# Which of two products of the last feed-forward group is split once more, on one Trainium2 core

## The chip, the cores and the metric

The kernel runs on one core of one Trainium2 chip. The core has a matrix engine (TensorE, "PE" in the profile), a vector engine (VectorE, DVE), a scalar engine (ScalarE, ACT), GpSimd (POOL) and SyncE (SP); each runs its own instructions in order, and the engines wait for each other by semaphores. SP, POOL and ACT also issue DMA transfers (rows SPq, POOLq, ACTq). Matrix products land in PSUM, eight banks of 128 x 512 fp32 numbers; everything else lies in SBUF. The metric is the device time of one execution in microseconds.

## The reference

A block with modulated layer norms, linear attention and a gated feed-forward part, for 2048 tokens of width 1024 and a hidden width of 3584:

```python
mod = (_silu(c) @ w_mod).reshape(c.shape[0], 6, 1, -1)   # sa, ca, ga, sb, cb, gb
h = _layernorm(x, axis=-1) * (1 + ca) + sa
x = x + ga * _A_ref(h, A_wqkv, A_wo)                     # linear attention
h = _layernorm(x, axis=-1) * (1 + cb) + sb
x = x + gb * _B_ref(h, B_w_gate, B_w_up, B_w_down)       # gelu(h @ w_gate) * (h @ w_up) @ w_down
```

The change lies in the last product, with w_down (3584 x 1024), and the outputs made from it.

## The kernel before, in words

**Stages.** `kvq_phase`, `merge_phase` and `wo_phase` make the attention part. Then the feed-forward part works on two groups of 1024 tokens: `gate_up(0)`, `down_out(0)`, `gate_up(1)`, `down_out(1)`. Each product of that part is a 2 x 2 block product made from seven products of half-size blocks (the Winograd form of Strassen's scheme), so sums of blocks take the place of an eighth product.

**The seven down products.** `down_out(g)` multiplies blocks of the hidden layer (A11, A12, A21, A22 and sums of them, 14 tiles of 128 x 512 each) with blocks of w_down or sums of them, named b11, b21, b22, t0, t1, t2, t3. The sums t0 to t3 lie in DRAM (`t_scr`). A *plain* product (`plain`) has four row tiles q of 128 tokens; each takes 14 matmuls of 512 columns into bank q (0 to 3), and is followed by its output step. b11, t1, t2, t3 are accumulated in these banks one onto the other, so that bank q holds the running sum. A *nested* product (`nested`) is itself made from seven smaller ones, steps g1 to g7, each of 2 x 7 matmuls of 256 columns into one of the banks 4 to 7; ACT copies the bank to SBUF after g1, g3 and g5 (`fcopy`), since the next step accumulates onto the bank, and DVE combines the copies with other banks. The outputs come in four quadrants (row pair r, column half c) after g2 (0,0), g5 (1,1), g6 (1,0) and g7 (0,1). Nested are b21, b22, t0 in both groups, and in group 1 also t2.

**The end of group 1 before.** t2 is nested. Its outputs P7 are kept in SBUF (`p7v`, helper `c22_last`) and subtracted from `p5v` to give the output block C22. Then t3 is plain, accumulated onto the running sum in the banks 0 to 3, and `c21_out` adds `p7v` to give C21. The steps of n7 (nested t2), n3 (nested b22) and m4 (plain t3) are interleaved by hand:

```python
run(n7[0], n3[5], n7[1], n3[6], *n7[2:5])
run(m4[6], n7[5], m4[7], m4[8], n7[6], *m4[9:], *m4[:6])
```

(even entries of m4 are matmuls of a row tile, odd ones its output.) Row tile 1 is the last, in two halves of 256 columns, each with its output and its store.

**An output** (`finish`, and the `out` helpers) is three DVE operations on a 128 x 512 tile: add or subtract with the PSUM bank, multiply by the gate row, add to the residual x, which was loaded into one of two buffers (`rest`, `xio_ring`; the load waits for the stores of the buffer's previous contents). A store to DRAM follows (`store`), issued by ACT in group 1 and by POOL in group 0.

**Sums on DVE.** `sub_sums` makes the four sums of a nested product's left side. The right sides' sums are made in `gate_up`: `wd_sums` in group 0 (t1, t3 and the second-level sums of b21, b22, t0, kept in `u_scr`) and `wd_late_sums` in group 1, for the fourth nested product. They are put between the DVE work of the 14 units of `gate_up` and *paced* to it.

**What sets the order.** The code records all operations; `Plan.order` then orders each engine's instructions. TensorE keeps the recorded order. For DVE, ACT, POOL and SP a list scheduler with fixed costs sweeps forward and back 16 times and keeps the best order it finds, for the whole program at once. So an edit at the end can move instructions anywhere on these four engines. In `down_out(0)` the second of two DMA transposes that load the next group's tokens (`h2_load`) is held back until the matmuls of nested t0 are done (`plan.hold`). ScalarE scales these tokens afterwards (`h2_mod`).

Of the kernel before, what the change touches and what calls it, by code (L numbers as in the profile page):

```python
# [266 lines left out]
def kernel(  # L267
# [97 lines left out]
    def at(off, shape, dt):  # L365
        return Ring(off, shape, dt, 1)()
# [95 lines left out]
    p7v = at(88, [TT, NW], FP32)  # L462
    c0_ring = Ring(174, [TG], F16, 3)
    gl_ring = Ring(177, [TG], F16, 3)
    c1_ring = Ring(180, [TG], F16, 3)
# [52 lines left out]
    def tt_op(out, a, b, op):  # L518
        ve.tensor_tensor(out=out, in0=a, in1=b, op=op)  # L519
# [250 lines left out]
    def fcopy(ring, ps):  # L770
        t = ring()
        ac.activation(out=t, in_=ps, func=AF.Copy)  # L772
        return t
# [209 lines left out]
    def move(dst, src, add):  # L983
# [5 lines left out]
    NESTED = ("b21", "b22", "t0", "t2")  # L989
# [43 lines left out]
    def wd_late_sums(c):  # L1033

        t, u = wdt_ring(), wdu_ring()[:, 0]
        sy.dma_start(out=t, in_=wd_full["t2"][:, 2 * c:2 * c + 2, :])
# [225 lines left out]
    def gate_up(g):  # L1262
# [33 lines left out]
        for i in range(NPR):  # L1296
# [54 lines left out]
            if i + 2 < NPR:  # L1351
# [2 lines left out]
    W_AT = [{"b11": 0, "b21": (4, 5, 6, 7, 8, 9, 10), "t0": (11, 12, 13, 0, 1, 2, 3), "t1": 4,  # L1354
# [3 lines left out]

    def down_out(g):
        NC = 2  # L1360
# [19 lines left out]
        def plain(name, A, out, start):  # L1380

            wt = quarters(W_AT[g][name], [NPR, NW], F16 if name[0] == "t" else BF16)
            sy.dma_start(out=wt, in_=wd_full[name])

            def mm(q, c):
                for i in range(NPR):
                    te.matmul(psm[:, q, c], lhsT=A[:, i, q * P:(q + 1) * P], rhs=wt[:, i, c],  # L1387
                              start=(start and i == 0), stop=(i == NPR - 1), skip_group_check=True)

            steps = []  # L1390
            for q in range(TT):
                parts = 2 if last and name == "t3" and q == 1 else 1
                for n in range(parts):
                    c = slice(n * NW // parts, (n + 1) * NW // parts)
                    steps += [lambda q=q, c=c: mm(q, c), lambda q=q, c=c: out(q, psm[:, q, c], c)]
            return steps

        def sub_sums(A, S, keep, cuts):
# [8 lines left out]
                tt_op(s4, x12, s2, ALU.add)  # L1407
                tt_op(s3, x11, x21, ALU.subtract)

        def nested(name, A, S, keep, out):  # L1410


            j, x = NESTED.index(name), A.rearrange("p (k e) t -> p e k t", e=2)
            at_w = W_AT[g][name]
            dt = F16 if name[0] == "t" else BF16
            y11, y21, y22 = (quarters(at_w[n], [NPR // 2, HB], dt) for n in (0, 1, 6))
            t1, t0, t2, t3 = (quarters(at_w[n], [NPR // 2, HB], F16) for n in (2, 3, 4, 5))
            for t, src in ((y11, wd_quarter(name, 0, 0)), (y21, wd_quarter(name, 1, 0)), (t1, u_scr[:, :, j, 1, :]),
                           (t0, u_scr[:, :, j, 0, :]), (t2, u_scr[:, :, j, 2, :]), (t3, u_scr[:, :, j, 3, :]),
                           (y22, wd_quarter(name, 1, 1))):  # L1420
                sy.dma_start(out=t, in_=src)
            x11, x12, x21, x22 = (x[:, e, :, h * HB:(h + 1) * HB] for h in range(2) for e in range(2))
            s1, s2, s4 = S
            s3 = x21 if keep is None else keep
            st = {}

            def mm(b, a, y, start):
                ps = psm[:, b, :].rearrange("p (q n) -> p q n", q=2)
                for q in range(2):
                    for k in range(NPR // 2):  # L1430
                        te.matmul(ps[:, q, :], lhsT=a[:, k, q * P:(q + 1) * P], rhs=y[:, k, :],  # L1431
                                  start=(start and q == 0 and k == 0), stop=(k == NPR // 2 - 1), skip_group_check=True)
                return ps

            def g1():
                st["a"] = free.pop(0)
                st["p1"] = fcopy(sub_ring, mm(st["a"], x11, y11, True))

            def g2():
                b = free.pop(0)  # L1440
                out(0, 0, mm(b, x12, y21, True), st["p1"], ALU.add)
                free.append(b)

            def g3():
# [64 lines left out]
        def u2_out(xt):  # L1509
            def out(q, ps, c):  # L1510
                t = w12[:, q, :]
                v = p5v[:, q, :] if last else t
                tt_op(v, p5v[:, q, :], ps, ALU.subtract)
                tt_op(t, v, gbrow[:, NW:D], ALU.mult)
                tt_op(t, t, xt[:, q, :], ALU.add)
            return out

# [20 lines left out]
        def c22_last(xt):  # L1538
            def out(r, c, ps, sb, op):
                t, p7 = f16_pair(), quad(p7v, r, c)  # L1540
                if sb is None:
                    ac.activation(out=p7, in_=ps, func=AF.Copy)
                else:
                    tt_op(p7, ps, sb, op)
                tt_op(t, quad(p5v, r, c), p7, ALU.subtract)
                tt_op(t, t, gate2(1, c), ALU.mult)
                tt_op(quad(xt, r, c), t, quad(xt, r, c), ALU.add)
                if (r, c) in ((1, 0), (0, 1)):
                    store(xt, 1, 1, 2 * r, 2 * r + 2)
            return out  # L1550

        def c21_out(xt):
            def out(q, ps, c):
                finish(xt, 1, 0, q, ps, p7v[:, q, c] if last else None, ALU.add, c)
                if last:
                    store(xt, 1, 0, q, q + 1, c)
                elif q % 2:
                    store(xt, 1, 0, q - 1, q + 1)
            return out

        def run(*steps):
# [42 lines left out]
        m7 = plain("t2", A21, c22_out(xo), False)  # L1604
        t2_load = plan.ops[-1]
        plan.hold(n5_done)
        plan.ahead = 36000
        h2_load(g + 1, 1)
        plan.ahead = 14000
        plan.hold()  # L1610
        plan.pairs.append((t2_load, plan.ops[-1]))
        for f in h2_mods[g + 1][1] + h2_steps:
            f()
# [37 lines left out]
```

## Time and profile before

| | |
|---|---|
| median of 7 runs | 760.17 us (759.39 to 761.46) |
| the profiled execution | 759.93 us, of which the span of instructions is 758.1 us |
| PE busy | 742.1 us (98%), 3955 matmuls |
| DVE busy | 607.8 us (80%) |
| ACT busy | 381.2 us (50%) |
| POOL busy | 103.7 us (14%) |
| TensorE clock granted | 1.000 |
| DMA | 149.81 MB, 197 GB/s over the span |
| matmul groups at stake | L1387 (plain) x402, 86.9 us; L1431 (nested) x686, 76.8 us |

The page gives busy times, a view of the span in 40 slices, DMA queues, the chain of work that ended last, and groups of instructions. A line number such as L1431 is that of the code, L519 is the helper `tt_op` (nearly all of DVE's work), L772 the helper `fcopy`. In a row of the timeline stand the start, the duration, the engine and line, the operation, what it writes and reads, a count, and in brackets the idle time before it and what ended it.

### The profile page before, as it was taken

To read this page: it belongs to the slowest core of one execution; us is meant where nothing else is said; L and a number is where in the kernel's file an instruction comes from. 1 tells how busy PE (TensorE), PEld (TensorE's weight loads), DVE (VectorE), ACT (ScalarE), POOL (GpSimd) and SP (SyncE) were. 2 spreads that over 40 slices of the span, in tenths; PEclk is the share of its full clock that TensorE was granted. 3 is DMA by queue.
4 is the path that set the end of the run, shared out by engine and by line. 5 is a ranking of instruction groups with operands and counts; after the bars stand their busy time and mean duration, and the time that the engine had idled before them with its cause. 6 is when DMAs were issued, how large, how long until landed. Compare 5 with 4: busy or idle time off the path is not lost.

```text
span 758.1 us, 10837 instructions
## 1 busy us (share of the span) xinstructions
PE 742.1 (98%) x3955; PEld 372.8 (49%) x3975; DVE 607.8 (80%) x1132; ACT 381.2 (50%) x581; POOL 103.7 (14%) x203
## 2 busy tenths in 40 slices
PE   6999999999999999999999999999999999999997
PEld 2444545454444444444444486544444444447684
DVE  7798996579997776899999787677686778777966
ACT  2665666668866668775444213314445454431010
POOL 2312323007121121231000000110000000000000
PEclk9999999999999999999999999999999999999999
DMA  9848257879489644698568699862332336698942
GB/s 310 300 112 213 99 134 166 307 277 163 129 257 263 201 154 140 206 319 279 170 234 276 183 252 304 260 193 78 89 106 62 112 98 182 200 271 255 326 142 84
DMA packets 177702, 149.81 MB, mean 198 GB/s; under 512 B 34225, under 2 KB 156593, under 8 KB 177009
## 3 DMA queue, kind: packets, MB, share of 16 engines
q1 hardware_dynamic: 160832, 115.03, 51.4%
q0 software_dynamic: 14464, 31.99, 13.9%
q10 hardware_dynamic: 2352, 2.10, 0.8%
q8 instruction: 31, 0.51, 0.3%
q14 instruction: 23, 0.18, 0.1%
HBM read 115.02 MB, written 34.08 MB: 197 GB/s over the span
## 4 chain that ended last, share of the span: by engine, by line
PE 57%; issue 23%; DMA 8%; DVE 5%; ACT 4%; POOL 1%; SPq 1%; POOLq 0%; DVEq 0%
PE psum L1259 17%; PE psum L1431 8%; PE psum L827 8%; PE psum L1387 7%; PE psum L1178 7%; DVE mem L519 5%; PE psum L897 4%; PE psum L926 4%; DMA mem<-xhs 2%; DMA us<-mem 2%; DMA mem<-in_A_wqkv_dram 2%; DMA mem<-in_A_x_dram 1%; DMA mem<-in_B_w_up_dram 1%; PE psum L941 1%; ACT mem L956 1%
## 5 line engine op out<-in xcount | busy, mean ns | idle before, releaser
L1259 PE MATMUL psum<-mem 128*128 128x512 f16 x1568 | 339.5, 379 | 2.2 <-DVE mem L519 2.2
L519 DVE TENSOR_TENSOR mem<-mem 128x512 f16<-128x512 f16 (+12 forms) x530 | 284.0, 566 | 36.6 <-DMA us<-mem 5.3
L519 DVE TENSOR_TENSOR mem<-psum,mem 128x512 f16<-128x512 f32 (+4 forms) x286 | 207.5, 744 | 87.2 <-ACT mem L772 59.3
L1259 PEld LDWEIGHTS <-mem 128*128 128x128 f16 (+1 forms) x1568 | 153.4, 98 | 188.0 <-issue 3.6
L772 ACT ACTIVATE mem<-psum 128x512 f32<-128x512 f32 (+1 forms) x207 | 129.6, 630 | 175.2 <-PE psum L1259 92.0
L1278 ACT ACTIVATE mem<-mem 128x512 f16<-128x512 f16 x84 | 52.8, 629 | 73.8 <-DVE mem L519 73.8
L1387 PE MATMUL psum<-mem 128*128 128x512 f16 (+2 forms) x402 | 86.9, 372 | 0.7 <-DVE mem L519 0.5
L1431 PE MATMUL psum<-mem 128*128 128x256 f16 (+1 forms) x686 | 76.8, 273 | 0.8 <-ACT mem L772 0.8
L1431 PEld LDWEIGHTS <-mem 128*128 128x128 f16 x686 | 67.1, 98 | 11.3 <-issue 1.1
L827 PE MATMUL psum<-mem 128*128 128x512 f16 (+1 forms) x272 | 61.6, 379 | 0.4
L1387 PEld LDWEIGHTS <-mem 128*128 128x128 f16 x406 | 39.7, 98 | 43.2 <-issue 0.7
L1178 PE MATMUL psum<-mem 128*128 128x512 f16 x256 | 57.2, 379 | 0.5 <-ACT mem L867 0.3
L897 PE MATMUL psum<-mem 128*128 128x512 f16 x224 | 51.1, 379 | 0.0
L827 PEld LDWEIGHTS <-mem 128*128 128x128 f16 x280 | 27.1, 98 | 31.1
L1178 PEld LDWEIGHTS <-mem 128*128 128x128 bf16 x256 | 25.0, 98 | 30.7 <-issue 0.6
L897 PEld LDWEIGHTS <-mem 128*128 128x128 f16 (+1 forms) x224 | 21.4, 97 | 26.6 <-issue 1.7
L597 DVE BATCH_NORM_STATS2 mem<-mem 128x6 f32<-128x512 bf16 x48 | 30.7, 673 | 0.4 <-DMA mem<-in_A_x_dram 0.2
L926 PE MATMUL psum<-mem 128*128 128x512 bf16 x126 | 29.7, 380 | 0.8 <-DVE mem L712 0.8
L984 POOL DMA_DIRECT2D ts<-in_B_w_down_dram x28 | 26.1, 1459 | 1.8 <-DMA ts<-in_B_w_down_dram 1.4
L1042 POOL DMA_DIRECT2D us<-mem x7 | 3.8, 544 | 155.6 <-DVE mem L519 155.6
L857 ACT ACTIVATE mem<-mem 128x1024 f16<-128x1024 f16 x18 | 19.0, 1054 | 11.6 <-DVE mem L519 11.5
L1158 ACT ACTIVATE mem<-mem 128x512 f16<-128x512 f16 x28 | 20.5, 802 | 8.1 <-DMA mem<-xhs 8.1
(123 smaller groups left out, 470.6 us busy)
## 6 DMA issues: line engine op xcount, KB each, us to landing
mem<-in_B_w_gate_dram SPq DMA_DIRECT2D x28, 512.0 KB, 4.0
mem<-in_B_w_up_dram SPq DMA_DIRECT2D x28, 512.0 KB, 5.5
mem<-us SPq DMA_DIRECT2D x28, 448.0 KB, 7.3
mem<-in_w_mod_dram SPq DMA_DIRECT2D x24, 512.0 KB, 7.2
mem<-ts SPq DMA_DIRECT2D x5, 1792.0 KB, 9.3
mem<-in_A_x_dram SPq DMA_DIRECT2D x32, 256.0 KB, 4.1
ts<-in_B_w_down_dram POOLq DMA_DIRECT2D x28, 256.0 KB, 6.7
us<-mem POOLq DMA_DIRECT2D x7, 768.0 KB, 7.2
```

Source lines behind the costliest of these rows:

```text
L519: ve.tensor_tensor(out=out, in0=a, in1=b, op=op)
L597: ve.bn_stats(out=stats[:, cb, :], in_=xt[:, cb * BW:(cb + 1) * BW])
L772: ac.activation(out=t, in_=ps, func=AF.Copy)
L827: te.matmul(ps, lhsT=A[:, k, i * P:(i + 1) * P], rhs=B[:, k, :], start=(start and k == 0), stop=(k == KH - 1), skip_group_check=True)
L897: te.matmul(o, lhsT=W[:, k, (j0 + i) * P:(j0 + i + 1) * P], rhs=h_form(a, k), start=(start and k == 0), stop=(k == KH - 1), skip_group_che ...
L926: te.matmul(ps, lhsT=hr1[b][:, k, tl * P:(tl + 1) * P], rhs=Wk[:, k, n * NW:(n + 1) * NW], start=(k == 0), stop=(k == KD - 1))
L984: gp.dma_start(out=dst, in_=src, **(dict(accum_op=ALU.add) if add else {}))
L1178: te.matmul(psw[:, half, :], lhsT=pqT[b][:, g, tl * P:(tl + 1) * P], rhs=Wp[:, g, half * NW:(half + 1) * NW], start=(g == 0), stop=(g == K ...
L1259: te.matmul(ps, lhsT=a[:, u, k, :], rhs=b[:, k, :], start=(start and k == 0), stop=(k == KH - 1), skip_group_check=True)
L1278: ac.activation(out=t, in_=src, func=AF.Gelu_apprx_tanh)
L1387: te.matmul(psm[:, q, c], lhsT=A[:, i, q * P:(q + 1) * P], rhs=wt[:, i, c], start=(start and i == 0), stop=(i == NPR - 1), skip_group_chec ...
L1431: te.matmul(ps[:, q, :], lhsT=a[:, k, q * P:(q + 1) * P], rhs=y[:, k, :], start=(start and q == 0 and k == 0), stop=(k == NPR // 2 - 1), s ...
```

## The change

In group 1 t2 becomes plain and t3 nested, and t3 comes last. (Groups 0 and 1 still have the same three other nested products; pacing and the held transpose stay as they are.) In detail:

- Nested t2's row of `W_AT` is replaced: t2 is loaded whole into slots 15 to 18, and t3 in seven quarters; `wd_late_sums` reads t3.
- Plain t2 accumulates onto the running sum in banks 0 to 3. Its output `c22_out` gives C22 from `p5v` and the bank; before that, ACT copies the bank into `u3v`.
- Nested t3 starts fresh. Its outputs are added to `u3v`, in `c21_last`, to give C21. Its DVE sums (`sub_sums`) are taken of A22 in place of A21.
- With `ends`, the last step g7 is made in two halves of 128 rows and 256 columns, each in a bank of its own (c and d), with an output and a store each; the subtraction u3 - bank of g5 is made earlier, in two operations, and the output of (1,1) is a step of its own (`g5_out`). One subtraction of each half of g7's output is done ahead, on SBUF alone.
- Plain products are no longer split, and `u2_out` no longer keeps the difference in `p5v`.
- In group 0 only the place of recording changes: the load of x for t3 and the load of t3 are recorded before the second half of plain t2.

```diff
@@ W_AT, group 1
-             "b22": (5, 0, 6, 7, 8, 9, 10), "t2": (15, 16, 17, 18, 11, 12, 13), "t3": 1}]
+             "b22": (5, 0, 6, 7, 8, 9, 10), "t2": 15, "t3": (1, 2, 3, 4, 11, 12, 13)}]
@@ nested(..., ends=False)
+            def mm_tile(b, a, y, start, q):
+                for k in range(NPR // 2):
+                    te.matmul(psm[:, b, 0:HB], lhsT=a[:, k, q * P:(q + 1) * P], rhs=y[:, k, :],
+                              start=(start and k == 0), stop=(k == NPR // 2 - 1), skip_group_check=True)
+                return psm[:, b, 0:HB]
...
             def g4():
                 st["c"] = free.pop(0)
-                mm(st["c"], s1, t0, True)
+                if ends:
+                    st["d"] = free.pop(0)
+                    for q in range(2):
+                        mm_tile(st["cd"[q]], s1, t0, True, q)
+                else:
+                    mm(st["c"], s1, t0, True)
             def g5():
-                u3 = fcopy(sub_ring, mm(st["a"], s3, t2, False))
-                out(1, 1, psm[:, st["c"], :].rearrange("p (q n) -> p q n", q=2), u3, ALU.subtract)
+                st["u3"] = fcopy(sub_ring, mm(st["a"], s3, t2, False))
+                if ends:
+                    for q in range(2):
+                        tt_op(st["u3"][:, q, :], psm[:, st["cd"[q]], 0:HB], st["u3"][:, q, :], ALU.subtract)
...
+            def g5_out():
+                out(1, 1, st["u3"], None, None)
...
             def g7():
-                out(0, 1, mm(st["c"], s4, y22, False), st["u2"], ALU.subtract)
+                if not ends:
+                    out(0, 1, mm(st["c"], s4, y22, False), st["u2"], ALU.subtract)
+                else:
+                    for q in range(2):
+                        out(0, 1, mm_tile(st["cd"[q]], s4, y22, False, q), st["u2"][:, q, :], ALU.subtract, q)
-            return [g1, g2, g3, g4, g5, g6, g7]
+            return [g1, g2, g3, g4, g5, *([g5_out] if ends else []), g6, g7]
@@ c22_out
+                if last:
+                    ac.activation(out=u3v[:, q, :], in_=ps, func=AF.Copy)
                 finish(xt, 1, 1, q, ps, p5v[:, q, :], ALU.subtract)
@@ c21_last (new; q is None for a quadrant, 0 or 1 for a half of g7)
+                if sb is None:
+                    tt_op(t, ps, u, ALU.add)
+                elif q is None:
+                    tt_op(sb, ps, sb, op)
+                    tt_op(t, sb, u, ALU.add)
+                else:
+                    tt_op(sb, u, sb, op)
+                    tt_op(t, ps, sb, ALU.add)
+                tt_op(t, t, gate2(0, c) if q is None else gbrow[:, cs], ALU.mult)
+                tt_op(x, t, x, ALU.add)
...
@@ the end of down_out
-        if last:
-            sub_sums(A21, sub_a, None, [slice(0, NPR // 2)])
-            n7 = nested("t2", A21, sub_a, None, c22_last(xo))
-            run(n7[0], n3[5], n7[1], n3[6], *n7[2:5])
-            m4 = plain("t3", A22, c21_out(rest(1, 0)), False)
-            run(m4[6], n7[5], m4[7], m4[8], n7[6], *m4[9:], *m4[:6])
-            return
...
-        run(*m7[:2], n3[5], *m7[2:4], n3[6], *m7[4:])
-        run(*plain("t3", A22, c21_out(rest(1, 0)), False))
+        run(*m7[:2], n3[5], *m7[2:4], n3[6])
+        if last:
+            sub_sums(A22, sub_a, None, [slice(0, NPR // 2)])
+            n4 = nested("t3", A22, sub_a, None, c21_last(rest(1, 0)), True)
+            run(*m7[4:6], *n4[:3], *m7[6:], *n4[3:])
+        else:
+            run(*m7[4:], *plain("t3", A22, c21_out(rest(1, 0)), False))
```

More of the change, by code (lines that the diff above doesn't have):

```diff
@@ L461 @@
     p1v, p5v = at(158, [TT, NW], FP32), at(166, [TT, NW], FP32)
-    p7v = at(88, [TT, NW], FP32)
+    u3v = at(88, [TT, NW], FP32)
     c0_ring = Ring(174, [TG], F16, 3)
@@ L988 @@
                **{f"t{j}": t_scr[:, j] for j in range(4)}}
-    NESTED = ("b21", "b22", "t0", "t2")
+    NESTED = ("b21", "b22", "t0", "t3")
     def wd_quarter(name, kh, h):
@@ L1035, in wd_late_sums @@
         t, u = wdt_ring(), wdu_ring()[:, 0]
-        sy.dma_start(out=t, in_=wd_full["t2"][:, 2 * c:2 * c + 2, :])
+        sy.dma_start(out=t, in_=wd_full["t3"][:, 2 * c:2 * c + 2, :])
         q11, q12, q21, q22 = (t[:, e, h * HB:(h + 1) * HB] for e in range(2) for h in range(2))
@@ L1391, in plain @@
             for q in range(TT):
[L1392 to L1395, printed above, removed]
+                c = slice(0, NW)
+                steps += [lambda q=q, c=c: mm(q, c), lambda q=q, c=c: out(q, psm[:, q, c], c)]
             return steps
@@ L1408, in sub_sums, with nested @@
                 tt_op(s3, x11, x21, ALU.subtract)
-        def nested(name, A, S, keep, out):
+        def nested(name, A, S, keep, out, ends=False):
             j, x = NESTED.index(name), A.rearrange("p (k e) t -> p e k t", e=2)
@@ L1448, in g4 @@
                 st["c"] = free.pop(0)
-                mm(st["c"], s1, t0, True)
-            def g5():
-                u3 = fcopy(sub_ring, mm(st["a"], s3, t2, False))
-                out(1, 1, psm[:, st["c"], :].rearrange("p (q n) -> p q n", q=2), u3, ALU.subtract)
+                if ends:
[4 more added lines that the diff above has]
+                    mm(st["c"], s1, t0, True)
+            def g5():
+                st["u3"] = fcopy(sub_ring, mm(st["a"], s3, t2, False))
[3 more added lines that the diff above has]
+                else:
+                    out(1, 1, psm[:, st["c"], :].rearrange("p (q n) -> p q n", q=2), st["u3"], ALU.subtract)
+            def g5_out():
+                out(1, 1, st["u3"], None, None)
             def g6():
@@ L1511, in out @@
                 t = w12[:, q, :]
-                v = p5v[:, q, :] if last else t
-                tt_op(v, p5v[:, q, :], ps, ALU.subtract)
-                tt_op(t, v, gbrow[:, NW:D], ALU.mult)
+                tt_op(t, p5v[:, q, :], ps, ALU.subtract)
+                tt_op(t, t, gbrow[:, NW:D], ALU.mult)
                 tt_op(t, t, xt[:, q, :], ALU.add)
@@ L1536, in c22_out, with c21_last, out @@
             return out
[L1538 to L1550, printed above, removed]
         def c21_out(xt):
             def out(q, ps, c):
-                finish(xt, 1, 0, q, ps, p7v[:, q, c] if last else None, ALU.add, c)
-                if last:
-                    store(xt, 1, 0, q, q + 1, c)
-                elif q % 2:
+                finish(xt, 1, 0, q, ps, None, None, c)
+                if q % 2:
                     store(xt, 1, 0, q - 1, q + 1)
+            return out
+        def c21_last(xt):
+            def out(r, c, ps, sb, op, q=None):
+                cs = slice(c * HB, (c + 1) * HB)
+                if q is None:
+                    t, u, x = f16_pair(), quad(u3v, r, c), quad(xt, r, c)
+                else:
+                    t, u, x = c0_ring()[:, 0:HB], u3v[:, q, cs], xt[:, q, cs]
+                if sb is None:
[3 more added lines that the diff above has]
+                    tt_op(t, sb, u, ALU.add)
+                else:
+                    tt_op(sb, u, sb, op)
+                    tt_op(t, ps, sb, ALU.add)
+                tt_op(t, t, gate2(0, c) if q is None else gbrow[:, cs], ALU.mult)
+                tt_op(x, t, x, ALU.add)
+                if q is None:
+                    store(xt, 1, 0, 2 * r, 2 * r + 2, cs)
+                else:
+                    store(xt, 1, 0, q, q + 1, cs)
             return out
@@ L1596, in down_out @@
         xo = rest(1, 1)
-        if last:
-            sub_sums(A21, sub_a, None, [slice(0, NPR // 2)])
-            n7 = nested("t2", A21, sub_a, None, c22_last(xo))
-            run(n7[0], n3[5], n7[1], n3[6], *n7[2:5])
-            m4 = plain("t3", A22, c21_out(rest(1, 0)), False)
-            run(m4[6], n7[5], m4[7], m4[8], n7[6], *m4[9:], *m4[:6])
-            return
[L1604 to L1613, printed above, removed]
-        run(*m7[:2], n3[5], *m7[2:4], n3[6], *m7[4:])
-        run(*plain("t3", A22, c21_out(rest(1, 0)), False))
+        m7 = plain("t2", A21, c22_out(xo), False)
+        if not last:
+            t2_load = plan.ops[-1]
+            plan.hold(n5_done)
+            plan.ahead = 36000
+            h2_load(g + 1, 1)
+            plan.ahead = 14000
+            plan.hold()
+            plan.pairs.append((t2_load, plan.ops[-1]))
+            for f in h2_mods[g + 1][1] + h2_steps:
+                f()
+        run(*m7[:2], n3[5], *m7[2:4], n3[6])
+        if last:
+            sub_sums(A22, sub_a, None, [slice(0, NPR // 2)])
+            n4 = nested("t3", A22, sub_a, None, c21_last(rest(1, 0)), True)
+            run(*m7[4:6], *n4[:3], *m7[6:], *n4[3:])
+        else:
+            run(*m7[4:], *plain("t3", A22, c21_out(rest(1, 0)), False))
     wo_phase(merge_phase(kvq_phase()))
```

## The prediction

> **What bounds the kernel now.** I read the page first, then the chain of waits from 700 us on, then the timeline of the end, engine by engine, and last TensorE's waits over the span. The page's first row:
>
> ```profile
> PE 742.1 (98%) x3955; PEld 372.8 (49%) x3975; DVE 607.8 (80%) x1132; ACT 381.2 (50%) x581; POOL 103.7 (14%) x203
> ```
>
> TensorE leaves 16 us of the 758.1 us span: about 9 at the start, 3.6 after its last matmul, the rest in waits. So what counts is the number of matmuls, TensorE's waits, and the tail. The chain at the end, and the pitch of matmuls in it (start, us, what):
>
> ```profile
> 720.27 18.34 PE psum L1431 x168
> 738.61 3.02 PE psum L1387 x14
> 741.63 1.53 PE psum L1431 x14
> ...
> 752.77 1.70 PE psum L1387 x14
> ...
> 755.28 0.29 DVE mem L519
> ```
>
> A matmul of 256 columns takes 0.1092 us (18.34/168), one of 512 takes 0.2157 (3.02/14). Now the end on DVE and TensorE:
>
> ```profile
> 743.83 1.61 DVE L519 TENSOR_TENSOR mem<-mem 128x512 f16<-128x512 f32 x3 [2.15 <-ACT mem L1542]
> 745.36 0.68 DVE L519 TENSOR_TENSOR mem<-mem,psum 128x512 f16<-128x512 f32 x1
> 746.07 0.88 DVE L519 TENSOR_TENSOR mem<-mem 128x512 f16<-128x512 f16 x2
> 746.87 0.68 DVE L519 TENSOR_TENSOR mem<-mem,psum 128x512 f16<-128x512 f32 x1
> ...
> 752.30 0.42 DVE L519 TENSOR_TENSOR mem<-mem,psum 128x256 f16<-128x256 f32 x1
> 752.75 0.62 DVE L519 TENSOR_TENSOR mem<-mem 128x256 f16<-128x256 f16 x2
> 752.77 1.69 PE L1387 MATMUL psum<-mem 128*128 128x256 f16 x14 [0.51 <-DVE mem L519]
> ...
> 754.50 0.42 DVE L519 TENSOR_TENSOR mem<-mem,psum 128x256 f16<-128x256 f32 x1 [1.13 <-PE psum L1387]
> 754.95 0.62 DVE L519 TENSOR_TENSOR mem<-mem 128x256 f16<-128x256 f16 x2
> ```
>
> Read starts, since durations overlap. An output of 128x512 costs DVE 1.51 us from PSUM (745.36 to 746.87) and 1.53 from SBUF (743.83 to 745.36); one of 128x256 costs 1.07 (754.50 to 755.57), its first operation 0.45. TensorE waits 0.51 once, since both halves of row tile 1 share a bank. After TensorE's end (754.46) one small output is left, and DVE stops at 755.57; the last store takes the span to 758.1, 2.53 later.
>
> **The matmuls.** From the first step of n7 on (T0 = 738.61 - 98 x 0.1092 = 727.91) there were 154 matmuls of 256 columns and 42 of 512; now there are 126 and 56: 28 x 0.1092 less, 14 x 0.2157 more, **-0.04**. The 0.51 wait goes too, as c and d are two banks.
>
> **The new end.** In the changed order TensorE runs t2 row 0, n3 g6, row 1, n3 g7, row 2, n4 g1 to g3, row 3, n4 g4 to g7. g5 ends at T0 + 98 x 0.1092 (n3's 28 and 70 of n4) + 56 x 0.2157 = 750.69. Nothing stands between g5 and g6, and g6 accumulates onto the bank that ACT copies. After n3's g5 that copy began 0.10 after the last matmul (728.01) and took 0.60, and DVE followed 0.03 later. So at 751.42 g6 starts (a new TensorE wait of **0.73**), and only then can DVE begin what hangs on g5. Its queue from there:
>
> - two subtractions u3 - bank, 0.45 each: 0.90. This shape (128x256, fp32 out) has no row. Between the fp16 one of 256 (0.29) and the fp32 one of 512 (0.72) they cost 0.58 to 1.44; I take the PSUM row of 256, the nearest.
> - output (1,1) from SBUF 1.53; output (1,0) after g6 1.51; two halves of (0,1), 1.07 and 0.02 between: 2.16.
>
> Sum 6.10: DVE ends at 757.52. TensorE is done at 754.65 (two steps of 1.53 and 0.16 to drain), so DVE sets the end, queued behind itself. Against 755.57 that is **+1.95**; the store behind it is the same size. [...]
>
> **What is late next.** All that DVE does before 751.42 must be out of the way. t2's row 3 ends at 747.64; ACT copies the bank to `u3v` first and DVE waits for that: 748.37 to 749.88. Free by 1.5 us. The copies of rows 0 to 2 lie beside TensorE work. The output of n4 g2 needs x in the second buffer, whose load waits for the store after n3 g7: TensorE 737.01, DVE behind row 1's output 738.83, store issued 738.86, load 2.35 later (as 736.30 to 738.65 before) at 741.21. Loads of this kind took 3.8 (at 476.73), 7.0 and 8.7 us to land, the latter two under saturated DMA (about 320 GB/s); here DMA carries 0 to 354 GB/s from one us to the next, so 3.8: 745.0, when DVE gets there (745.03). Up to 747.0 it would cost nothing. [...]
>
> Loads of t2 (whole) and t3 (quarters) need slots that t0, b21 and t1 leave by 704 to 720 us; 8.4 to 10.4 us of landing end long before 727.9 and 740: nothing. t2's DVE sums go, t3's four take their place.
>
> **Moved elsewhere.** The scheduler reorders all queues, so earlier waits change. Two views show them, TensorE's waits over the span and the timeline around 480 us:
>
> ```profile
> PE psum L1259 <- DVE mem L519: 2.2, 4, 0.7
> ```
>
> ```profile
> 478.82 0.81 ACT L1158 ACTIVATE mem<-mem 128x512 f16<-128x512 f16 x1 [4.83 <-DMA mem<-xhs]
> 479.54 0.57 ACT L772 ACTIVATE mem<-psum 128x512 f32<-128x512 f32 x1
> ```
>
> ```profile
> 461.32 0.84 SPq L1421 DMA_DIRECT2D mem<-us  x1
> 462.71 0.99 SPq L1383 DMA_DIRECT2D mem<-ts  x1
> 463.75 0.43 SPq L1421 DMA_DIRECT2D mem<-in_B_w_down_dram  x1
> 464.27 12.29 SPq L1116 DMA_TRANSPOSE mem<-xhs  x1
> ```
>
> - SP, group 0. ACT's copy after n3 g5 stood behind a scaling that waited for the transpose, and TensorE lost 0.78 for it. Now the quarter of w_down (448 KB) is issued behind the transpose, so less lies ahead of it: at 316 to 459 GB/s 1.0 to 1.4 us. The `us` load moves behind `ts`, which may issue the transpose 0.3 later. Bounds -0.78 to +0.3; I take **-0.4**. The quarter, at 476.6, lands 3.8 (the load at that place) to 11.2 us (itself before) later, at 480.4 or 487.8; TensorE wants it at 484.7: 0 to +3.1, taken as 0.
> - SP, start of gate_up(1). The first w_up tile goes behind the x load: issued 494.6, not 478.3. In 4.0 to 6.6 us it is there by 501.2; TensorE needs it at 505.2, and its sums wait on DVE without TensorE waiting: 0.
> - DVE in gate_up. Group 0's units 7, 8 and 10 hold the waits of 0.43, 0.35 and 0.74: the additions that free a bank stood behind ten paced sums. Now one of each pair goes ahead, while the second in unit 8 has a 0.64 operation more before it: -0.1 together. In gate_up(1) the additions go ahead by 0.5 to 1.7 us of DVE work and a wait of 0.71 shrinks: -0.4. Bounds -2.2 (all waits go) to +1.5 (as much again as group 0 has); I take **-0.5**.
> - One sum of the attention part (0.69) goes earlier while DVE is 97% busy (40 to 60 us): 0 to +0.69, taken as 0. POOL only swaps neighbours.
>
> **Sum.** 1.95 - 0.4 - 0.5 = **+1.05 us** on the profiled execution's 759.93: 760.98. That execution lies 0.24 below the median of 760.17, so the forecast is **761.2 us**. A measurement of this kernel can tell about 0.2%, 1.5 us, from no change: 758.65 to 761.69 is "the same".
>
> **Rivals.**
>
> - *Nothing is given back.* The tail costs 1.95 and the reordered queues win nothing: 762.1. For it: the gains rest on a schedule of the same kind. Against: TensorE's wait at 480 has one cause that the new order eases. Chance 0.25, slower.
> - *The x load lands late, and ACT's queue passes it on.* Place: the output of n4 g2. ACT's queue then holds that output's store, the `u3v` copy of row 3, the store of C22 and g5's copy, in this order, and each waits for DVE's step before it. From landing L: 0.42 + 0.41 + 0.66 + 1.51 + 0.41 + 0.63 = 4.0, so it decides beyond L = 747.4, that is 6.2 us after issue. With 7.0 and 8.7 us g5's copy ends 0.8 and 2.5 late, giving 762.0 to 763.7, or 762.9 to 764.6 with nothing given back. For it: ACT did hold a copy behind a wait at 479.54. Against: quiet DMA. Chance 0.11, slower.
> - *The tail is cheaper or more waits go.* If TensorE set the end, with one small output after 754.65, the tail would cost 0.2 and the time be 759.5; if all waits of gate_up went besides, 757.8. For it: DVE has idle time before 751. Against: 6.1 us of DVE work hang on g5's copy, whatever came before. Chance 0.14, half of it beyond 0.2% faster.
>
> **Numbers.** The forecast, within 760.4 to 761.7, has 0.50. Same 0.50 + 0.07; slower 0.25 + 0.11; faster 0.07. The range 759.2 to 762.9 leaves out most of the last rival below and the dearer half of the late load above.
>
> **What would show it.** Right: DVE ends about 2.9 us after TensorE, without idle time from g5's copy on; TensorE waits 0.7 before g6 for L772; the last x load lands within 5.8 us. Wrong: a DVE wait on DMA near 745; TensorE ending last; waits at 480 and in gate_up unchanged or greater than 3 us in all.

## The result, and the profile after

The changed kernel takes 763.22 us (median of 13 runs, 761.41 to 764.85) against 760.21 us for the kernel before beside it (33 runs, 758.69 to 761.88). The ratio is **1.0038, 95% interval 1.0029 to 1.0046**: 2.2 to 3.5 us slower. The forecast was 761.2, within 759.2 to 762.9. The profiled execution took 762.05 us, its span 760.3.

First the page's busy row. PE is as busy as before (742.1 then) with 14 matmuls less, DVE too; the time is in waits and in the tail.

```profile
PE 742.5 (98%) x3941; PEld 371.4 (49%) x3961; DVE 607.6 (80%) x1134; ACT 381.0 (50%) x584; POOL 104.0 (14%) x203
```

Then the timeline of the end (start, duration, engine and line). g5 is the row at 749.41, its copy ends 0.03 before 751.83, and from there DVE has no idle time until 757.72, 2.66 behind TensorE's end (755.06):

```profile
749.41 1.69 PE L1437 MATMUL psum<-mem 128*128 128x256 f16 x14
751.83 0.75 DVE L519 TENSOR_TENSOR mem<-psum,mem 128x256 f32<-128x256 f32 x2 [1.51 <-ACT mem L772]
751.84 1.69 PE L1437 MATMUL psum<-mem 128*128 128x256 f16 x14 [0.74 <-ACT mem L772]
752.61 1.61 DVE L519 TENSOR_TENSOR mem<-mem 128x512 f16<-128x512 f32 x3
753.37 1.69 PE L1429 MATMUL psum<-mem 128*128 128x256 f16 x14
754.14 0.68 DVE L519 TENSOR_TENSOR mem<-psum,mem 128x512 f16<-128x512 f32 x1
...
757.10 0.62 DVE L519 TENSOR_TENSOR mem<-mem 128x256 f16<-128x256 f16 x2
```

This is the tail of the prediction: DVE has 5.89 us of work behind g5's copy, where 6.10 was predicted. What the prediction did not have stands in TensorE's waits over the span (total, times, longest):

```profile
PE psum L1259 <- DVE mem L519: 2.4, 3, 1.6
...
PE psum L536 <- ACT mem L956: 0.9, 1, 0.9
PE psum L1437 <- ACT mem L772: 0.7, 1, 0.7
```

The last is g6's. The one on L956 was 0.2 before; it lies at 182 us, in the attention part, whose code the change doesn't touch. Here are ScalarE and TensorE around it, in the kernel before and then in the changed one:

```profile
179.82 1.02 ACT L956 ACTIVATE mem<-psum 128x1024 bf16<-128x1024 f32 x1
180.74 1.02 ACT L772 ACTIVATE mem<-psum 128x1024 f32<-128x1024 f32 x1
180.89 1.91 PE L536 MATMUL psum<-mem 128*32 128x512 bf16 x32 [0.19 <-ACT mem L956]
```

```profile
179.07 1.00 ACT L772 ACTIVATE mem<-psum 128x1024 f32<-128x1024 f32 x1
179.97 1.08 ACT L954 ACTIVATE psum<-psum,mem 128x1024 f32<-128x1024 f32 x1
181.08 1.02 ACT L956 ACTIVATE mem<-psum 128x1024 bf16<-128x1024 f32 x1
182.16 1.91 PE L536 MATMUL psum<-mem 128*32 128x512 bf16 x32 [0.92 <-ACT mem L956]
```

The scheduler has put a copy (L772) of 0.9 us ahead of the pair L954 and L956, for which TensorE waits.

**Theory.** The tail has 1.8 to 1.9 us of the 3.0; the rest is the scheduler's new order of everything ahead of it, above all in the attention part. **Rivals:** the tail has all of it and the new order costs nothing; and, within the tail, TensorE's 0.74 wait costs, not DVE's queue.

### The profile page after: what moved, and what is told of

Same layout as the page of the kernel before. It is cut to its first block, busy times and chain, and to the rows that moved or that the text cites. A ratio compares the mean times of both kernels' runs of the same rounds, so it can differ in the third digit from the quotient of the medians.

```text
span 760.3 us, 10818 instructions
## 1 busy us (share of the span) xinstructions
PE 742.5 (98%) x3941; PEld 371.4 (49%) x3961; DVE 607.6 (80%) x1134; ACT 381.0 (50%) x584; POOL 104.0 (14%) x203
## 4 chain that ended last, share of the span: by engine, by line
PE 55%; issue 23%; DMA 7%; DVE 5%; ACT 5%; SPq 2%; POOL 1%; POOLq 0%; DVEq 0%; ACTq 0%
PE psum L1259 17%; PE psum L1437 8%; PE psum L1387 7%; PE psum L1178 7%; PE psum L827 7%; PE psum L897 4%; DVE mem L519 4%; PE psum L926 3%; DMA us<-mem 2%; SPq L1116 2%; DMA mem<-in_A_wqkv_dram 2%; DMA mem<-x2s 1%; DMA mem<-in_A_x_dram 1%; PE psum L941 1%; DMA mem<-in_B_w_up_dram 1%
## 5 line engine op out<-in xcount | busy, mean ns | idle before, releaser
L519 DVE TENSOR_TENSOR mem<-mem 128x1024 f16<-128x1024 bf16 (+12 forms) x530 | 282.0, 564 | 27.7 <-ACT mem L956 5.3
L519 DVE TENSOR_TENSOR mem<-psum,mem 128x512 f16<-128x512 f32 (+5 forms) x289 | 209.4, 739 | 87.7 <-ACT mem L772 58.4
L772 ACT ACTIVATE mem<-psum 128x512 f32<-128x512 f32 (+1 forms) x207 | 128.7, 630 | 163.6 <-PE psum L1259 86.8
L1387 PE MATMUL psum<-mem 128*128 128x512 f16 (+1 forms) x388 | 86.8, 379 | 0.2
L1437 PE MATMUL psum<-mem 128*128 128x256 f16 (+1 forms) x658 | 74.4, 273 | 0.7 <-ACT mem L772 0.7
L1437 PEld LDWEIGHTS <-mem 128*128 128x128 f16 x658 | 64.4, 98 | 11.3 <-issue 0.9
L827 PE MATMUL psum<-mem 128*128 128x512 f16 (+1 forms) x272 | 61.6, 379 | 0.4
L1387 PEld LDWEIGHTS <-mem 128*128 128x128 f16 x392 | 38.4, 98 | 43.5
L1178 PE MATMUL psum<-mem 128*128 128x512 f16 x256 | 57.2, 379 | 0.5 <-ACT mem L867 0.3
L827 PEld LDWEIGHTS <-mem 128*128 128x128 f16 x280 | 27.1, 98 | 31.1
L1178 PEld LDWEIGHTS <-mem 128*128 128x128 bf16 x256 | 25.0, 98 | 30.7 <-issue 0.6
L926 PE MATMUL psum<-mem 128*128 128x512 bf16 x126 | 30.2, 380 | 1.0 <-DVE mem L712 0.7
```

The source lines that it names most:

```text
L827: te.matmul(ps, lhsT=A[:, k, i * P:(i + 1) * P], rhs=B[:, k, :], start=(start and k == 0), stop=(k == KH - 1), skip_group_check=True)
L926: te.matmul(ps, lhsT=hr1[b][:, k, tl * P:(tl + 1) * P], rhs=Wk[:, k, n * NW:(n + 1) * NW], start=(k == 0), stop=(k == KD - 1))
L1178: te.matmul(psw[:, half, :], lhsT=pqT[b][:, g, tl * P:(tl + 1) * P], rhs=Wp[:, g, half * NW:(half + 1) * NW], start=(g == 0), stop=(g == K ...
```

## The experiments

To part order from code, `Plan.order` is replaced by a list of operations written out (TensorE's list is always its own):

```diff
+FIXED_ORDER = "..."
...
     def order(self):
-        best = None
...
-        return [self.ops[n] for _, n in best[1]]
+        raw = zlib.decompress(base64.b85decode(FIXED_ORDER))
...
+        return [self.ops[n] for n in got]
```

The edit of an experiment is then which list stands in which stretch. Lists can be mixed like this, since TensorE's order is the same in both kernels up to the end of gate_up(1).

### Tail and order apart (a1 to a4)

```diff
  code of            | attention | gate_up(0) | down_out(0), gate_up(1) | down_out(1)
- before             | before    | before     | before                  | before
+ a1_tail_alone      | before    | before     | before                  | after   (code of after)
+ a2_order_alone     | after     | after      | after                   | before
+ a3_attention_order | after     | before     | before                  | before
+ a4_best_order      | before    | before     | after                   | before
```

> The changed kernel with its order written out: every engine's instructions stand in the order of before up to the end of gate_up(1) (matched one by one), and from there in the changed kernel's own. So only the new tail is in it. My theory: of the 3.0 us that were measured, the tail has 1.8 (29.41 us from T0 to DVE's end, against 27.66) and the rest comes from the new order of everything ahead of it; so +1.8 us here, ratio 1.0024, with TensorE's waits in the attention part and gate_up as before (waits near 182 us 0.2, not 0.9; the 0.78 near 480 us back). Rival: the order ahead of the tail is worth nothing and the tail has all of it: +3.0, ratio 1.004.

> The other half: the kernel before, its code unchanged, with its order written out: up to the end of gate_up(1) every engine's instructions stand as in the changed kernel, and from there as before. My theory: +1.2 to +1.4 us (attention part +2.0, gate_up(0) +0.56, the transpose's wait -0.78, gate_up(1) -0.41), ratio 1.0017. Rival: no difference, 1.000, if the tail has all of it.

> The kernel before, with the changed kernel's order up to the first matmul of gate_up(0) alone, and its own order from there. My theory: this is the step that my prediction took as nothing: +2.0 us, ratio 1.0026, with TensorE's 0.9 wait near 182 us for ACT's pair of L954 and L956 and some 0.6 more between 36 and 52 us. Rival: a sum more or less in that stretch is hidden, 0 to +0.4, ratio 1.0000 to 1.0005.

> The kernel before, with its own order up to the end of gate_up(0), the changed kernel's order from there to the end of gate_up(1) (the transpose issued ahead of the quarter of w_down, the additions that free banks ahead of the paced sums), and its own order for the last down products. My theory: -0.78 - 0.41 = -1.2 us, ratio 0.9984. Rival: these waits come back elsewhere (w_down's quarter lands late, or the sums of the fourth nested product are late): 0, ratio 1.000.

Each result gives the median, the ratio to the kernel before and, in brackets, its 95% interval; a difference in us is the ratio less 1, times the time of before. Measured, against 760.26: a1 762.9, ratio 1.0029 (1.0018 to 1.0041); a2 761.12, 1.0007 (0.9997 to 1.0017); a3 761.89, 1.0025 (1.0015 to 1.0035); a4 759.30, 0.9988 (0.9978 to 0.9999). The tail alone costs 2.2, the attention order 1.9; the middle gains 0.9. The order as a whole is not distinguished from nothing in a2, where 1.9 - 0.9 was to be expected, +1.0: within its interval. By these times a1 and a2 leave the first rival standing, since a1's interval reaches +3.1 and a2's includes no change. It falls by a3, where order alone costs, and by the profiles, in which the tail takes 1.87 more in five of five (the table below), not 3.0.

### The tail (b1, b2)

```diff
@@ b1, c21_last: the DVE operations of output (1,0) left out
                 cs = slice(c * HB, (c + 1) * HB)
+                if (r, c) == (1, 0): return store(xt, 1, 0, 2 * r, 2 * r + 2, cs)
@@ b2, the end of down_out(1)
-            run(*m7[4:6], *n4[:3], *m7[6:], *n4[3:])
+            run(n4[0], *m7[4:6], n4[2], *m7[6:], *n4[3:5], n4[1], *n4[5:])
```

> The run 'tail alone' (2.2 us above before, measured) with the three DVE operations of n4's output (1,0) left out, so that this quadrant of C21 is stored as the residual x alone. My theory: after g5's copy DVE is the end, one operation behind the other without idle time, so leaving out one output of 1.5 us ends it 1.4 to 1.5 us earlier: +0.7 to +0.8 us against before, ratio 1.001, DVE about 1.2 us behind TensorE's end. Rival: TensorE's 0.74 wait ahead of g6 and the longer chain through the bank set the end, and DVE only follows: then +2.2 stays, DVE still 2.7 behind TensorE.

> The run 'tail alone' with the steps of n4 in another order: g1, row tile 2 of t2, g3, row tile 3, g4, g5, g2, g6, g7. TensorE has 1.53 us of g2 to do while ACT copies g5's bank, so its 0.74 wait goes; but output (0,0) then stands in DVE's queue behind g5 too. My theory: DVE's queue is the end, and it now has 7.5 us (two subtractions 0.78, three outputs of 1.5, two halves 2.16) from 1.5 us earlier on: DVE ends as before or 0.3 earlier, +1.9 to +2.2 against before, although TensorE ends 0.74 earlier. Rival: TensorE's wait is what the tail costs, 0.74 goes with it: +1.4 us.

b1 760.70, 1.0007 (0.9993 to 1.0021); b2 764.15, 1.0047 (1.0033 to 1.0062), against 760.11. In b1's profile DVE ends 1.34 behind TensorE, though g6's wait of 0.74 is still there. These are TensorE's last row and DVE's last one:

```profile
752.12 1.69 PE L1429 MATMUL psum<-mem 128*128 128x256 f16 x14
...
754.53 0.62 DVE L519 TENSOR_TENSOR mem<-mem 128x256 f16<-128x256 f16 x2
```

In b2's, TensorE runs from g5 on without a wait, and DVE ends 4.16 behind it:

```profile
749.95 4.75 PE L1437 MATMUL psum<-mem 128*128 128x256 f16 x42
752.36 0.76 DVE L519 TENSOR_TENSOR mem<-psum,mem 128x256 f32<-128x256 f32 x2 [1.51 <-ACT mem L772]
...
759.76 0.62 DVE L519 TENSOR_TENSOR mem<-mem 128x256 f16<-128x256 f16 x2
```

From the start of down_out(1) to DVE's end, before takes 81.03 us, the changed kernel 82.91, b1 81.58, b2 83.37. TensorE's wait is gone in b2 and nothing is won, and b1 wins 1.3 of the tail with the wait in place: the second rival falls. That b2's tail is even later than I expected (by 0.5) is because output (0,0) has four DVE operations (2.2 us), not three. Its time is 1.4 above a1's; what lies beyond the tail's 0.5 is not explained (b2 has five runs). DVE's queue behind g5's copy is the tail's cost.

### A cheaper end (b3, b4, d3)

```diff
@@ b3, b4, d3: code of before, the end of down_out(1)
-            run(m4[6], n7[5], m4[7], m4[8], n7[6], *m4[9:], *m4[:6])
+            run(m4[6], n7[5], m4[7], m4[8], n7[6], *m4[9:], *m4[2:4], *m4[:2], *m4[4:6])
@@ b4 also: the changed kernel's order in down_out(0) and gate_up(1), as in a4
@@ d3 also: SP's queue in down_out(0), one swap (c3: SP's whole order of that stretch)
-L1421 DMACopy mem<-in_B_w_down_dram 128x7x256
 L1116 DmaTransposeAnt mem<-xhs_1_100 128x8x512
+L1421 DMACopy mem<-in_B_w_down_dram 128x7x256
```

> The kernel before (its own order up to the end of gate_up(1)) with the two halves of row tile 1 of t3 apart: row 3, then row 1's first half, row 0, row 1's second half, in place of row 0 and the two halves after each other. The halves share a bank, and TensorE waited 0.51 between them for DVE. My theory: the wait is on the path, TensorE ends 0.5 earlier and so does all: -0.5 us, ratio 0.9993. Rival: DVE, which now has row 0's output of 1.1 to 1.5 us just ahead of the last half's, gives it back: 0.

> The best of what the runs have shown, on the code of before: its order up to the end of gate_up(0), the changed kernel's order from there to the end of gate_up(1) (measured alone: -0.9 us), and the halves of the last row tile apart (-0.5 expected). My theory: they add up, -1.4 us, ratio 0.9982. Rival: the halves give nothing: -0.9.

> The kernel before with halves of the last row tile apart and one swap on SP: the transpose ahead of the quarter of w_down, with the loads behind it (x for t3's output, w_up's first tile) left in before's order. SP's whole order alone was 2.3 slower, since w_up's tile went behind the load of x while DVE's order still had the sum on w_up first (DVE waited 3.6 us for that load). My theory: so the swap alone keeps the gain at 480 us, TensorE's wait of 0.8 to 1.7 there goes, nothing is lost at the start of gate_up(1): with the halves' 0.67, -1.4 us, ratio 0.998. Rival: the quarter, now 12 us later, is late for g7 or delays what follows it: -0.7 or worse.

b3 759.89, 1.0003 (0.9989 to 1.0016), b4 758.83, 0.9990 (0.9977 to 1.0003), against 760.11; d3 758.59, **0.9980 (0.9965 to 0.9995)**, against 760.30. b3 alone shows no gain in its time, though its tail is shorter by 0.67 in the profile, in b4 and d3 too (80.36 and 80.37 against 81.03); it is smaller than the interval. b4's interval holds both its theory (-1.4) and its rival (-0.9). d3 is the version that beats both kernels.

### The attention order taken apart (c1, c2, d1)

```diff
@@ c1: ScalarE's order of the attention part alone (3 places), c2: VectorE's alone (75 operations elsewhere)
@@ d1: two moves alone. VectorE
-L519 TensorTensor mem<-mem 128x1024
+L519 TensorTensor mem<-mem 128x1024 x2
 L748 TensorScalarPtr mem<-mem 128x512 x8
@@ d1, ScalarE
+L772 Activation mem<-psum 128x1024
 L954 Activation psum<-psum,mem 128x1024
 L956 Activation mem<-psum 128x1024
-L772 Activation mem<-psum 128x1024
```

> The kernel before with ScalarE's order of the attention part alone as in the changed kernel; three copies or exponentials have changed places with a neighbour, the last one the copy (L779 of the code as changed, L772 in its profile) that now stands ahead of the pair of L954 and L956 near 180 us. DVE, POOL and SP as before. The whole attention order cost 1.9 us (measured), of which the profile shows 0.5 to 0.7 as a wait of TensorE for L956 near 182 us. My theory: that wait comes with ScalarE's swap: +0.6 us, ratio 1.0008, and the wait in the trace. Rival: it comes from DVE, which feeds the pair later: 0.

> The kernel before with VectorE's order of the attention part alone as in the changed kernel (75 operations in other places, one sum of 0.69 us among them that goes ahead by a dozen places near 45 us). ACT, POOL and SP as before. My theory: the rest of the 1.9 us of that order, 1.0 to 1.3 us, ratio 1.0015. Rival: ScalarE's swap has all of it: 0 to +0.2.

> The kernel before with two operations moved and nothing else: on DVE the sum of 0.69 us (one of w_qkv's, wide 1024) ahead of the eight scalings of L748 near 45 us, 32 places earlier, and on ScalarE the copy L772 near 180 us ahead of the pair L954 and L956, two places earlier. My theory: these two are most of the attention order's 1.5 us: TensorE is 0.6 later from 51 us on and waits 0.7 to 1.1 for L956 near 182 us, +1.5 us in all, ratio 1.002. Rival: only the whole new order of 75 operations costs; two neighbours' moves are hidden: 0 to +0.3.

c1 761.57, 1.0015 (1.0002 to 1.0029), c2 761.27, 1.0014 (1.0000 to 1.0029), against 760.15; d1 761.71, 1.0021 (1.0010 to 1.0032), against 760.30. Counted from the start of the long row of L926 near 37 us, TensorE's first matmul of L941 comes 14.27 later in before, and 0.61 later still in every profile with VectorE's order or the one move (the changed kernel, a2, a3, c2, d1), never in one without. L926 uses the eight scalings of L748 one by one, as DVE delivers them (in d1 its weight loads wait for them eight times, 2.2 us in all), and these start 0.6 later behind the sum. TensorE and DVE, in the kernel before and then in the changed one:

```profile
37.31 14.44 PE L926 MATMUL psum<-mem 128*128 128x512 bf16 x63
46.91 2.67 DVE L748 TENSOR_SCALAR mem<-mem 128x512 f16<-128x512 f16 x8
```

```profile
36.75 15.04 PE L926 MATMUL psum<-mem 128*128 128x512 bf16 x63
46.95 2.66 DVE L748 TENSOR_SCALAR mem<-mem 128x512 f16<-128x512 f16 x8
```

The wait for L956 is 0.7 to 1.1 in every profile with ScalarE's order and 0.2 or less in the others. To the first matmul of `wo_phase` (L1178) before takes 153.97, c1 1.33 more, c2 1.00, a3, with both, 1.56, d1 1.49. The two moves do what the whole order does: in d1 0.60 comes near 50 us and 0.91 near 181. c1 and c2 add up to more than a3. A stretch that is late may hide part of the next wait; but profiles with the old order differ by 0.7 among themselves, so this isn't shown.

### SP's queue alone (c3)

> The kernel before with SP's order in down_out(0) alone as in the changed kernel: the load of t2 ahead of a load of sums, the transpose ahead of a quarter of w_down. DVE, ACT and POOL as before. My theory: the wait of TensorE near 480 us, 0.8 in the profile of before and 1.6 in that of the attention order alone, goes, and with it all that the order of the middle gains: -0.8 to -1.0 us, ratio 0.9988, and gate_up(1)'s order has nothing of it. Rival: half of the gain is gate_up(1)'s: -0.4.

c3 762.45, 1.0026 (1.0012 to 1.0040), against 760.15: a miss. The wait at 480 went, as expected, but gate_up(1) lost 2.9:

```profile
494.96 0.45 SPq L1248 DMA_DIRECT2D mem<-in_B_w_up_dram  x1
...
500.00 0.69 DVE L519 TENSOR_TENSOR mem<-mem 128x1024 f16<-128x1024 bf16 x1 [3.62 <-DMA mem<-in_B_w_up_dram]
...
508.14 170.24 PE L1259 MATMUL psum<-mem 128*128 128x512 f16 x780 [1.97 <-DVE mem L519]
```

SP's new order loads x ahead of w_up's first tile, and in DVE's old order the sum on that tile stands ahead of outputs that could go first. In the changed kernel DVE's order fits SP's. But about 1.7 of the 2.9, by the estimate at the end, is a lowered clock: behind the wait of 1.97 the granted clock is 0.50. Not all runs have it: six of c3's twelve have a mean clock of 0.997 or 0.998 and took 762.7 to 764.9, the other six 761.3 to 762.2, some 1.2 above before. An order of one queue is not a part that can be tried by itself; d3, with only the transpose moved, kept a gain.

### Does the sum close on the changed kernel? (d2, e1 to e3)

```diff
  code of                    | attention | gate_up(0) | down_out(0), gate_up(1) | down_out(1)
- after                      | after     | after      | after                   | after
+ d2, e2 (the same kernel)   | before    | after      | after                   | after
+ e1_after_old_to_422        | before    | before     | after                   | after
+ e3 (code of before)        | before    | after      | before                  | before
```

> The changed kernel with the order of before up to the first matmul of gate_up(0), and its own order from there. My theory: the +3.0 us of the change fall by the attention part's 1.5, to +1.5, ratio 1.002: the tail's 1.9 and a gain of 0.4 to 0.9 at the transpose. Rival: the parts don't add up, because a stretch that is late hides waits behind it: +2.2 to +3.0 as with the tail alone.

> The changed kernel with the order of before up to the end of gate_up(0), not only up to its first matmul, and its own order from there. The run with the old attention order (expected +1.5) took +3.8. Theory A: the new order of gate_up(0) costs where the attention part is early (in its profile one wait of 2.03 near 358 us, in place of three of 0.4 to 0.9): here it is gone, +1.3 (tail 2.2, order of the middle -0.9), ratio 1.0017. Theory B: the +3.8 of six runs was late landings of the transpose near 241 us (1.78 in its profile), which come by chance: here +1.3 to +2, and the repeated run below falls as well. Theory C: the tail and the order of the middle don't add up: +3 or more.

> The changed kernel with the old order of the attention part once more, beside its neighbours on one chip. Theory A (gate_up(0)'s new order costs): +1.3 plus what that order costs alone, +2 or more. Theory B (chance): +1.5. Theory C: +3.8 again, and the run beside it, with gate_up(0) in the old order too, as well.

> The kernel before with the changed kernel's order in gate_up(0) alone (all engines). In the profiles that stretch took 0.4 to 0.8 us more with the new order in three of three, and -0.4 to +1.9, 0.3 on the mean, with the old one in thirteen. Theory A: +1 to +2, ratio 1.002. Theories B and C: +0.3 or nothing.

d2 763.89, 1.0050 (1.0033 to 1.0066, six runs) against 760.30: a miss by far. e1 761.93, 1.0017 (1.0001 to 1.0033), e2 762.47, 1.0012 (0.9997 to 1.0026), e3 761.52, 1.0016 (0.9996 to 1.0035), all against 760.88. Repeated as e2, the kernel of d2 gives what the sum says, +0.9 with -0.2 to +2.0, and e1 gives +1.3 with +0.1 to +2.5. So theory C falls; d2's six runs were high. Its profile shows one reason, a transpose that landed late, and two of the six show another, a mean clock of 0.996 and 0.997, lower than in any run of the changed kernel (both at the end). e1, without the new order of gate_up(0), is no faster than e2 with it, and e3 leaves that order between -0.3 and +2.7: theory A is not settled by the times. Two of e3's twelve runs have a mean clock below 0.998 and took 764.9 and 767.5; the other ten took 761.3 on the mean, 0.6 above the like runs of before.

The profiles say more. In the new order TensorE has one wait of 1.65 to 2.59 near 357 us in five of five. In the old order it has waits of 0.2 to 1.4 at three places.

## Why the prediction failed

The time of each stretch in TensorE's timeline, over all profiles with the old and with the new order (or tail) there, in us:

| stretch | old: n, range, mean | new: n, range, mean | difference | predicted |
|---|---|---|---|---|
| attention, from L926 at 37 us | 13, 153.84 to 154.52, 154.06 | 3, 155.51 to 155.67, 155.57 | **+1.5** | 0 |
| gate_up(0) | 14, 170.86 to 173.17, 171.51 | 5, 171.61 to 174.14, 172.72 | +1.2 | -0.1 |
| down_out(0) | 10, 81.38 to 82.30, 81.76 | 7, 80.44 to 81.61, 80.85 | -0.9 | -0.4 |
| gate_up(1) | 10, 169.29 to 170.33, 169.65 | 7, 169.62 to 170.47, 169.96 | +0.3 | -0.4 |
| down_out(1) to DVE's end | 9, 81.03 to 81.04, 81.04 | 5, 82.90 to 82.92, 82.91 | **+1.87** | +1.95 |

(c1, c2 and d1 are left out of the first row, c3 and d3 of the third and fourth, b1 to b4 and d3 of the last.) Against +1.05 predicted, the rows give +4.0; `wo_phase` between the first two rows gives 0.5 back (16 old profiles, 3 new), and 0.7 of gate_up(0), by the estimate at the end, is a lowered clock in two of five profiles, neither of them that of the changed kernel. That leaves 2.8, within the 2.2 to 3.5 measured.

- *The tail, +1.95*: right, +1.87, with its mechanism. g6's wait is 0.74 (0.73 predicted); the two subtractions, which had no row, take 0.78 together (751.83 to 752.61), where 0.90 was taken. The first lasts 0.42, and the second starts 0.08 before the first has ended. The x load lands 3.3 us after its issue (3.8 was taken), and DVE doesn't wait for it.
- ***"One sum of the attention part (0.69) goes earlier ...: 0 to +0.69, taken as 0"***: this is the step that failed. The sum alone cost 0.61, near its upper bound. On an engine that the same sentence calls 97% busy (19.33 of the 20 us from 40 to 60) and on which TensorE waits, the operation that went ahead cost nearly its whole length; there was no ground for 0. And ScalarE's queue in that part has no term in the prediction: its copy ahead of L954 cost 0.7 to 0.9 more. The whole order cost 1.5, most of what the forecast of +1.05 lacks.
- *DVE in gate_up, -0.5*: no gain came. In gate_up(1) the wait of 0.71 that was to shrink is in the profiled execution of before but in few other profiles of the same order: in a3, b1, b2, b3, c2 and d1 the stretch is 0.9 shorter without any change. A gain was counted on a wait that comes and goes, and the +0.3 is within the spread of the old profiles. In gate_up(0) the new order pools three small waits into one large one.
- *The transpose, -0.4*: right in mechanism, too small: the stretch is 0.9 shorter. In d3 the one SP swap and the shorter tail gave 1.5 together, of which the tail has 0.67; with an interval of 1.1 to each side the swap's share is not measured closely. In the changed kernel the copy at 479.74 no longer makes TensorE wait:

```profile
465.06 11.85 SPq L1116 DMA_TRANSPOSE mem<-xhs  x1
476.95 0.58 SPq L1420 DMA_DIRECT2D mem<-in_B_w_down_dram  x1
...
479.02 0.81 ACT L1158 ACTIVATE mem<-mem 128x512 f16<-128x512 f16 x1 [3.66 <-DMA mem<-xhs]
479.74 0.57 ACT L772 ACTIVATE mem<-psum 128x512 f32<-128x512 f32 x1
```

- *The first w_up tile, 0*: held in the profiles of the changed kernel, a2, a4 and e2; in b4, e1 and d2, with the same order there, TensorE waits 0.4, 0.8 and 1.0 at the start of gate_up(1).
- The rival of the late x load has the measured 763.2 within its times (762.0 to 764.6), but what it rests on, a load that lands over 6.2 us after its issue, didn't happen: a hit by that way would have been luck. The rival "Nothing is given back" had 762.1, nearer than the forecast, also for a reason that it didn't name: it took the new order as harmless at worst.
- One count of the prediction is off without effect on its sum: of TensorE's 16 us without work in before, 6.5 lie in the first 32 us, not about 9 at the start.

What stays open: how much of gate_up(0)'s +1.2 is its order (0.5 without the lowered clock in the profiles, 0.6 by e3's runs without it, neither clear of the spread), and whether the 0.5 of `wo_phase` is more than chance.

## What to carry to other kernels

Where a scheduler orders the whole program, compare the order of every queue in every stretch, also far from the edit, and price each move by whose wait it feeds: here operations of 0.7 and 0.9 us, put ahead of the ones that the bound engine waits for, cost 0.6 and 0.7 to 0.9. A wait in one profiled execution that depends on when a transfer lands may not be there in the next: it is no gain until two or three profiles show it (the 0.71 in gate_up(1) was none). The last outputs were a queue on one engine here: count all that hangs on the last common event (5.9 us on one copy) before shortening the matrix engine's part.

## What the runs showed of the hardware

**Behind three waits of TensorE its granted clock was halved.** In e2 and e3 TensorE's wait near 357 us was 2.59 and 2.21, in c3 that at 508 us 1.97. The granted clock behind each was 0.50: in windows of 1 us it was 0.87, 0.50, 0.50, 0.50 and 0.92 from 356 to 361 us in e2, and 0.67, 0.50, 0.50 and 0.63 from 359 to 363 us in e3. That is 3.4 us at 0.50 in each of the two, and half of it, about 1.7, is my estimate of what it cost. In c3 the mean clock of 0.998 over a span of 761.8 us gives 1.5, about as much. First e2's matmuls behind the wait, then one window of e2 and one of c3 (length, PE busy, granted clock, DMA share, GB/s):

```profile
356.81 8.49 PE L1259 MATMUL psum<-mem 128*128 128x512 f16 x31 [2.59 <-DVE mem L519]
```

```profile
358.00:359.00 1.00, 1.00 (x4) 0.50 1.04 399
```

```profile
510.00:511.00 1.00, 1.00 (x4) 0.50 0.75 262
```

After waits of 2.20 (a2), 2.03 (d2) and 1.65 (the changed kernel) near 357 us the clock stayed at 1.00. So the length of the wait alone doesn't tell them apart: behind 1.97 us the clock was lower, behind 2.20 it was not. What does is not shown by these runs.

**The same transfer lands at different times.** In 14 profiles DVE waits for the second transpose of `wo_phase`, and it goes on 8.4 (c2) to 11.4 us (b3) behind the transpose's issue. In before the transpose is issued at 230.23 and lands after 8.8; DVE goes on at 239.09, and TensorE waits nothing for it. In b3, with the same instructions in that stretch, it is issued at 231.40 and lands after 11.4; DVE waits 3.47 for it, to 242.82, and TensorE then 1.59. In d2 DVE goes on after 10.2, having waited 3.12. Runs of one kernel differ by 3 us and more (the changed kernel's by 3.4); such draws, and those of the clock, are two reasons that the traces show.
